# A Fourier filter and a token-mixing block on one core: the first batch redone in its first stage and its transposes, the first group moved ahead, and the planner's time from engine to engine cut to a quarter

## The chip, the cores and the metric

One core of one Trainium2 chip runs the whole kernel. Times are device microseconds (us) of one execution; a smaller one is better. The time before is the median of three runs, 1521.86 us (1519.93 to 1523.29).

## What is computed

```python
# x: (8, 3136, 256) float32; filters (1569, 256); w_ch1 (256, 1024), w_ch2 (1024, 256)
X = np.fft.rfft(x, axis=1)                       # along the 3136 tokens
y = np.fft.irfft(X * (filt_r + 1j * filt_i), n=3136, axis=1).astype(np.float32)

X = np.fft.fft(np.fft.fft(y, axis=1), axis=2)    # along tokens, then along 256 channels
u = y + np.real(X).astype(np.float32)
un = (u - mean(u)) / np.sqrt(var(u) + 1e-06)     # over the channels
out = u + np.maximum(un @ w_ch1, 0.0) @ w_ch2
```

## The kernel before

Each of the 8 batches is a transform, and the transform's result feeds the products of the block. A token axis of 3136 is split 112 x 28, so that every transform step is a product of TensorE. To keep float32 accuracy, a float32 value is held as a float16 pair (high part and rest), and each float32 product is three float16 products (high x high, high x rest, rest x high).

The steps of one batch `b`, with the line numbers of the profile:

- `load_x`, `measure_x`, `weigh_x`: seven loads of 448 KB; VectorE takes the absolute maximum of each (L387); a scale `sx`, a power of two, follows by a transpose and a product of TensorE in float32 (L364, L381).
- `first`, 14 chunks: ScalarE scales and rounds to the high part (L533), VectorE makes the rest (L535), TensorE does three products of 512 columns (L544), ScalarE and VectorE split the result into a pair (L549, L551), and a DMA stores 224 KB to DRAM tensor `d` (L554).
- `load_at`, seven pieces `ch`: `d` comes back in another order (L577). For batch 0 the tables `s2` and `i1` of the next steps are loaded in between (L582, L585).
- `spectrum`, two halves `hf` per piece: 16 small products (L618, L619), the filter on VectorE (L630, L634), the complex sums on GpSimd or VectorE (L641, L644, L646), the split into a pair (L653, L656 or L659), and a DMA transpose of the pair into `z` (L663). For batch 0, ScalarE scales the filters first (`scale_filters`, L457 to L462).
- `fold`: sums and differences of the halves (L682, L696), kept as pairs in `eo` (L708, L711) for the transform along the channels.
- `inverse1`, two per piece: six products (L732 to L734), split (L741, L743), store to DRAM (L746).
- `load_b2`, `inverse2`, `bring`: load (L760), products (L779), scale (L792), store to DRAM tensor `dy` (L803, L807).

The tokens of all batches are then one row of 49 groups of 256. For group `g`, `fetch` loads `y` (L825), `prepare` mixes the channels (L860, into `mix`), adds the result to `y` on VectorE (L870), takes mean and variance (L948, L949) and the weights of the normalisation (L952 to L964); `normalize` writes `un` (L977), splits it (L982, and L985 on VectorE for the first two groups) and sends it through a DMA transpose into `ut` (L991). `products` then makes 8 steps per group: a product `h` of six matmuls (L1013), the rectifier and its split (L1041, L1043), and two steps later 12 matmuls into `acc` (L1054). In all there are 392 steps. `weight` and `split_weights` turn the float64 weights, loaded as words in eight pieces (L1096), into float32 on VectorE and ScalarE (L1119 to L1135) and then into pairs (L1159 to L1163).

The order of the instructions on each engine isn't written out. A planner (`Plan`) runs all these steps as tasks in a time of its own: each task names an engine and a length, waits for events or for a buffer of a ring (`take`, `give`), and the engine that is free takes the waiting task with the lowest order number. The engines then work through the orders that came out, strictly one after another. `HOP` is what the planner adds when a task goes from one engine to another; `brought`, `FIRST` and `gate` tie the steps of later batches and groups to a step of `products`. Rings stand for the PSUM banks: `psf` (4 banks), `psh` (2, for `h`) and `pso` (2, for `acc`).

## Time and profile before

| what | us |
|---|---|
| device time, median of three | 1521.86 |
| device time of the profiled execution | 1524.17 |
| its span, first to last instruction | 1522.4 |
| TensorE busy in the span | 1379.6 (91%) |
| VectorE busy | 1114.9 (73%) |
| ScalarE busy | 784.4 (52%) |
| GpSimd busy | 541.5 (36%) |
| first product `h` begins at | 179.06 |

The profile shows one execution. Its lines by stretch give the busy time of each engine in that stretch, the clock that the throttle granted to TensorE (1.00 is 2.4 GHz, 0.50 is 1.2 GHz, a number between is a mean of the two), and the mean busy share and rate of the DMA engines. A line of the order of time gives the start, the length, the engine, the line of the code, what was written and read, and in brackets how long the engine sat idle just before and who ended it.

### The profile page before, as it was taken

The numbers are of one execution on the slowest core, as the hardware profiler recorded it, in microseconds if no ns is written. First come the engines' busy times: TensorE is split into PE (matmuls) and PEld (weight loads), VectorE is DVE, ScalarE is ACT, GpSimd is POOL, SyncE is SP. The second block draws the span as 40 slices with busy tenths as digits, with TensorE's granted clock in tenths as the row PEclk, the third lists the DMA queues.
The fourth block names the chain that finished last, engine by engine and source line by source line (L and its number), as shares of the span: only waits on it lengthen the run. The fifth ranks groups of instructions, "written<-read, shape, count | busy, mean of one in ns | idle before, by whom it ended". The sixth has DMA issues, their size and how long they took to land.

```text
span 1522.4 us, 29999 instructions
## 1 busy us (share of the span) xinstructions
PE 1379.6 (91%) x11217; PEld 935.0 (61%) x11217; DVE 1114.9 (73%) x2409; ACT 784.4 (52%) x1450; POOL 541.5 (36%) x675
## 2 busy tenths in 40 slices
PE   3442599999999999999999999999999999999998
PEld 1341257765776567666666666666666677666666
DVE  6774977787787877888688867878778878465563
ACT  4543565455464655565555545465455646443442
POOL 4461046501671038400860057211760167210100
PEclk9555589999999999999999999999999999999999
DMA  7999497956988698948987599758997698735521
GB/s 214 207 211 220 126 197 165 241 144 175 220 189 198 170 211 172 263 123 197 226 178 213 144 214 214 218 138 192 210 196 197 163 218 181 179 83 124 132 68 43
DMA packets 419827, 273.12 MB, mean 179 GB/s; under 512 B 234048, under 2 KB 361072, under 8 KB 419680
## 3 DMA queue, kind: packets, MB, share of 16 engines
q1 hardware_dynamic: 419680, 271.19, 77.0%
q8 instruction: 88, 1.44, 0.4%
q14 instruction: 59, 0.48, 0.1%
HBM read 113.31 MB, written 102.76 MB: 142 GB/s over the span
## 4 chain that ended last, share of the span: by engine, by line
PE 56%; DVE 4%; DMA 2%; issue 2%; ACT 1%; SPq 1%; POOL 1%; ACTq 0%; POOLq 0%; DVEq 0%
PE acc L1054 23%; PE h L1013 23%; PE y L779 3%; PE s L544 2%; PE mix L860 2%; DVE y L870 1%; PE i L732 1%; PE i L734 1%; PE i L733 1%; DMA ut<-u 1%; PE s L618 1%; PE s L619 1%; DMA b<-d 1%; DVE st L948 1%; DVE h L1043 1%
## 5 line engine op out<-in xcount | busy, mean ns | idle before, releaser
L1054 PE MATMUL acc<-w2s,h 128*128 128x256 f16 x4704 | 591.9, 273 | 2.8 <-DVE y L1068 2.7
L1013 PE MATMUL h<-ut,w1s 128*128 128x512 f16 x2352 | 578.0, 382 | 16.1 <-DMA ut<-u 11.6
L1054 PEld LDWEIGHTS <-h 128*128 128x128 f16 x4704 | 452.0, 98 | 142.3 <-issue 18.8
L1041 ACT ACTIVATE h<-h 128x512 f16<-128x512 f32 x392 | 233.5, 596 | 482.7 <-PE h L1013 481.9
L1043 DVE SCALAR_TENSOR_TENSOR h<-h,h 128x512 f16<-128x512 f32 x392 | 268.3, 684 | 213.9 <-ACT h L1041 213.1
L1013 PEld LDWEIGHTS <-w1s 128*128 128x128 f16 x2352 | 228.4, 98 | 222.9 <-issue 19.6
L988 POOL TENSOR_TENSOR u<-un,u 128x512 f16<-128x512 f32 x94 | 109.6, 1167 | 598.4 <-ACT u L982 524.6
L870 DVE SCALAR_TENSOR_TENSOR y<-mix,alpha,y 128x508 f32<-128x508 f32 (+1 forms) x368 | 160.5, 475 | 38.6 <-PE mix L860 33.4
L544 PE MATMUL s<-x,s 112*112 112x512 f16 x336 | 100.3, 425 | 20.6 <-ACT x L533 9.7
L644 POOL TENSOR_TENSOR yt<-yt,t 128x224 f32<-128x224 f32 x105 | 70.2, 668 | 134.3 <-DVE yt L636 83.4
L977 ACT ACTIVATE un<-y,sb 128x256 f32<-128x256 f32 x196 | 110.7, 595 | 12.5 <-DVE sb L964 8.5
L659 POOL TENSOR_TENSOR y<-yt,y 128x448 f16<-128x448 f32 x105 | 109.6, 1048 | 18.7 <-ACT y L653 15.4
L630 DVE TENSOR_TENSOR yt<-s,ft 128x448 f32<-128x448 f32 x112 | 69.1, 617 | 32.2 <-PE s L619 29.3
L535 DVE SCALAR_TENSOR_TENSOR x<-x,sx,x 112x512 f16<-112x512 f32 x111 | 86.9, 808 | 6.4 <-ACT x L533 6.3
L732 PE MATMUL i<-z,i 112*112 112x256 f16 x224 | 65.5, 292 | 25.2 <-DMA z<-y 20.1
L551 DVE TENSOR_TENSOR ast<-s,ast 112x512 f16<-112x512 f32 x112 | 74.5, 684 | 15.3 <-ACT ast L549 14.9
L711 POOL TENSOR_TENSOR eo<-ef,eo 128x448 f16<-128x448 f32 (+6 forms) x62 | 59.7, 966 | 71.8 <-ACT eo L708 71.6
L387 DVE TENSOR_REDUCE mx<-x 112x1 f32<-112x1024 f32 x56 | 67.5, 1211 | 23.6 <-DMA x<-x 23.6
L743 DVE TENSOR_TENSOR bt<-i,bt 112x512 f16<-112x512 f32 x112 | 74.8, 684 | 13.6 <-ACT bt L741 13.3
L948 DVE BATCH_NORM_STATS2 st<-y 128x6 f32<-128x256 f32 x196 | 80.8, 412 | 3.0
L792 ACT ACTIVATE ys<-y,alpha 128x512 f32<-128x512 f32 x112 | 73.4, 685 | 18.2 <-PE y L779 18.0
L544 PEld LDWEIGHTS <-s 112*112 112x112 f16 x336 | 46.3, 143 | 56.6 <-issue 37.1
(130 smaller groups left out, 1609.8 us busy)
## 6 DMA issues: line engine op xcount, KB each, us to landing
x<-x SPq DMA_DIRECT2D x56, 448.0 KB
d<-ast SPq DMA_DIRECT2D x112, 224.0 KB
at<-d SPq DMA_DIRECT2D x56, 448.0 KB
d<-bt SPq DMA_DIRECT2D x112, 224.0 KB
b<-d SPq DMA_DIRECT2D x56, 448.0 KB
out<-y SPq DMA_DIRECT2D x98, 256.0 KB
y<-dy SPq DMA_DIRECT2D x92, 256.0 KB
dy<-ys SPq DMA_DIRECT2D x96, 224.0 KB
```

Source lines behind the costliest of these rows:

```text
L535: nc.vector.scalar_tensor_tensor(x16[:, 1], x, sx[:112, 1:2], x16[:, 0], op0=ALU.mult, op1=ALU.subtract)
L544: nc.tensor.matmul(p, s1[:, hs], x16[:, hx], start=i == 0, stop=i == 2)
L659: nc.gpsimd.tensor_tensor(y16[:, :, 1, :112], ytv, y16[:, :, 0, :112], op=ALU.subtract)
L732: nc.tensor.matmul(p[:, i], i1[:, j + i, 0], z[:, i, 0], start=True, stop=False)
L870: nc.vector.scalar_tensor_tensor(out, p, al, y, op0=ALU.mult, op1=ALU.add)
L948: nc.vector.bn_stats(st[:, 2 * t + k], y[:, t, k])
L977: nc.scalar.activation(un[:, k], y[:, t, k], AF.Identity, bias=sb[:, i, 1:2], scale=sb[:, i, 3:4])
L988: nc.gpsimd.tensor_tensor(u16[:, :, :, 1], unv, u16[:, :, :, 0], op=ALU.subtract)
L1013: nc.tensor.matmul(p.rearrange("p (t k q) -> p t k q", t=2, k=2), w1s[:, d, hw, 128 * f : 128 * f + 128], utv[:, :, :, d, hx], start=i == ...
L1041: nc.scalar.activation(h[:, 0], p, AF.Relu)
L1043: nc.vector.scalar_tensor_tensor(h[:, 1], p, 0.0, h[:, 0], op0=ALU.max, op1=ALU.subtract)
L1054: nc.tensor.matmul(acc[:, kind], h[:, hh, c0 : c0 + 128], w2s[:, f, hw], start=f == 0 and kind == 0 and i == 0, stop=f == 7 and kind == 1 ...
```

## The change

1. **The planner.** `HOP` is 0.1 where it was 0.4.
2. **First stage of batches 0 and 1 in float32** (`WIDE = 2`). TensorE multiplies the loaded `x` itself by a float32 table `s1f`, one product per chunk, and the scale is applied when the result is split. The split of `x` (L533, L535) goes for these two batches. Chunks of batch 0 no longer wait for the scale; six PSUM banks of `psf` and `pso` and twelve buffers take their results.
3. **Filters.** They are no longer scaled by ScalarE; the filter operation on VectorE takes the scale as its scalar. What stays is a change of sign of a part (`conjugate`). Six of the eight filter measurements are on ScalarE, four before.
4. **Spectra of batch 0 turned on TensorE.** Four float32 transposes per half go to PSUM, and ScalarE and VectorE split from there into `z`. The 14 DMA transposes of batch 0 go, and with them the split of the spectra in SBUF. The later batches keep theirs.
5. **Tables.** They are loaded when the first-stage stores of batch 0 have been issued, ahead of `at`.
6. **Group 0 and the weights.** Group 0 is mixed as soon as its spectra are there, is normalised tile by tile, and has `pso` banks and low order numbers. Weights are loaded from the first `at` pieces on, four of the eight straight into the space of `w1s` and `w2s`. Batch 1 gets its order by hand: its first stage from step -7 on, its spectra from step 9 on.

Cut to its core, the diff reads:

```diff
+WIDE = 2
-FILTERS_ON_ACT = (0, 3, 4, 6)
-RAW_IN = ("ys", "ys", "b2", "ut", "ut", "ys", "b2", "ys")
+FILTERS_ON_ACT = (0, 2, 4, 5, 6, 7)
+RAW_IN = (None, None, "ys", "ys", "ut", "ut", None, None)
-HOP = 0.4
+HOP = 0.1
...
     def first(b, q, t):
+        ring = ("psf", "psf", "psf", "psf", "pso", "pso")[q % 6] if b == 0 else "psf"
+        wide = b < WIDE
...
+        if wide:
+            yield "PE", 0.86 if b else 1.2
+            nc.tensor.matmul(p, s1f, x, start=True, stop=True)
...
+            yield until(("sx", b))
...
         yield "ACT", 0.53
+        if wide:
+            nc.scalar.activation(st[:, :, 0], p, AF.Copy, scale=sx[:112, 1:2])
...
+        if wide:
+            nc.vector.scalar_tensor_tensor(st[:, :, 1], p, sx[:112, 1:2], st[:, :, 0], op0=ALU.mult, op1=ALU.subtract)
...
+    def load_tables():
+        for ch in range(7):
+            yield until(("fnyq",), *((("stored", 0),) if ch > 1 else ()))
+            yield "SP", 0.75, -101 if ch < 2 else -79
+            nc.sync.dma_start(s2[:, 8 * ch : 8 * ch + 8], a["c_s2"][:, 8 * ch : 8 * ch + 8])
...
+            nc.sync.dma_start(i1[:, 4 * ch : 4 * ch + 4], a["c_i1"][:, 4 * ch : 4 * ch + 4])
...
+        def filtered(out, p, f):
+            nc.vector.scalar_tensor_tensor(out, p, pF[:, 1:2], f, op0=ALU.mult, op1=ALU.mult)
...
+        if b == 0:
+            kp = yield take("psh")
+            pt = spare(f"yT_{ch}_{hf}")[:112].rearrange("p (j c) -> p j c", j=4)
+            yield "PE", 1.2
+            for j in range(4):
+                nc.tensor.transpose(pt[:, j], yt[:, hf, 112 * j : 112 * j + 112], ident)
...
+            yield "ACT", 0.53
+            nc.scalar.copy(z[:, :, 0], pt)
+            yield "DVE", 0.64
+            nc.vector.tensor_tensor(z[:, :, 1], pt, z[:, :, 0], op=ALU.subtract)
...
+        if g == 0:
+            yield until(("spectrum", 0, 6, 0), ("spectrum", 0, 6, 1))
+            kp, pm = yield from mixing()
...
+            if g == 0:
+                yield from weigh(slice(2 * t, 2 * t + 2))
+                plan.spawn(normalize(g, t, y, sb, ut), -56 + t)
...
+        x0, t0, s0, piece, half = ((-280, -100, -80, PIECE, HALF), (-30, -7, 9, 0.9, 1.25))[b] if b < 2 else (0,) * 5
```

How the rows of the engines move at the places that matter is shown word for word. On SyncE, which issues all DMAs, the end of the first stage of batch 0 stood like this before (`ast` are the stored chunks, `s` and `i` the tables, `at` the pieces that come back):

```order
L554 DMA d_0_168<-ast_13_375 112x1024
L577 DMA at_0_188<-d_0_168 112x8x256
L585 DMA i_83<-c_i 112x896
L577 DMA at_1_210<-d_0_168 112x8x256
```

and it stands like this now:

```order
L561 DMA d_0_133<-ast_13_274 112x1024
L596 DMA s_83<-c_s 112x896
L600 DMA i_84<-c_i 112x896
...
L596 DMA s_83<-c_s 112x896
L589 DMA at_0_144<-d_0_133 112x8x256
L589 DMA at_1_151<-d_0_133 112x8x256
L589 DMA at_2_158<-d_0_133 112x8x256
```

Nine tables of 196 KB now stand between the last store and `at_0`, where none stood.

On VectorE, between the last split of the first inverse step (`bt_6_1`) and the first addition of group 0 (`y`), before:

```order
L743 TENSOR_TENSOR bt_6_1_1026<-i_0_6_1_1008,bt_6_1_1026 112x2x256
L1119 TENSOR_SCALAR cv_3_1038<-raw_1033 128x512
L1121 SCALAR_TENSOR_TENSOR w_1037<-raw_1033,cv_3_1038 128x512
...
L387 TENSOR_REDUCE mx_1134<-x_6_1025 112x1
L508 TENSOR_REDUCE mx_1134<-mx_1134 112x1
L870 SCALAR_TENSOR_TENSOR y_118<-mix_1187,alpha_379,y_118 128x4x127
```

and now:

```order
L781 TENSOR_TENSOR bt_6_1_1025<-i_0_6_1_1004,bt_6_1_1025 112x2x256
L1190 SCALAR_TENSOR_TENSOR w_992<-raw_418,cv_2_993 128x512
L1192 SCALAR_TENSOR_TENSOR w_992<-raw_418,w_992 128x512
L1188 TENSOR_SCALAR cv_3_1036<-raw_472 128x512
...
L390 TENSOR_REDUCE mx_117<-x_5_968 112x1
L386 COPY sw_1183<-pb_w_1184 128x2
L390 TENSOR_REDUCE mx_117<-x_6_1024 112x1
L912 SCALAR_TENSOR_TENSOR y_119<-mix_920,alpha_307,y_119 128x4x127
```

The weight conversions there are those of the last six pieces now (18 long operations and 5 short ones, beside the seven maxima of batch 1), where three pieces stood before and the rest came after that addition.

On TensorE, around the first product `h` (`s_1_q` are the first-stage chunks of batch 1), before:

```order
L860 MATMUL mix_1227<-mix,eo 128x127
L544 LDWEIGHTS s_81
L544 MATMUL s_1_0_1276<-x_1_0_1238,s_81 112x512
...
L544 MATMUL s_1_5_1356<-x_1_5_1307,s_81 112x512
L1013 LDWEIGHTS w1s
L1013 MATMUL h_0_1384<-ut_1319,w1s 128x512
```

and now:

```order
L902 MATMUL mix_1233<-mix,eo 128x127
L384 MATMUL pb_x_1286<-row_x_1280,ones 128x2
L534 MATMUL s_1_0_1299<-x_0_922,s1f 112x512
...
L534 MATMUL s_1_6_1353<-x_3_925,s1f 112x512
L534 MATMUL s_1_7_1372<-x_3_925,s1f 112x512
L1080 LDWEIGHTS w1s
L1080 MATMUL h_0_1343<-ut_1204,w1s 128x512
```

Eight chunks of batch 1 stand ahead of the first `h`, six before, and each is one float32 product instead of three float16 ones.

## Rows read from the trace of the kernel before

**Rows 1.** By stretch, all engines: length; busy (x) of PE, PEld, DVE, ACT, POOL; clock, DMA.

```profile
0.00:20.00 20.00, 0.93 (x3) 0.74 (x4) 9.71 (x15) 2.49 (x5) 2.99 (x12) 1.00 0.92 260
...
60.00:80.00 20.00, 7.57 (x108) 7.16 (x108) 17.86 (x33) 10.69 (x23) 16.90 (x22) 0.50 1.15 230
80.00:100.00 20.00, 11.36 (x112) 10.43 (x112) 15.66 (x26) 9.08 (x18) 15.89 (x20) 0.67 1.11 235
...
200.00:220.00 20.00, 20.00 (x161) 13.33 (x160) 13.56 (x36) 9.01 (x18) 6.26 (x8) 0.88 1.05 219
```

**Rows 2.** In order of time, first stage of batch 0: start, length, engine, line.

```profile
19.75 0.16 DVE L383 COPY sx<-pb_x 128x2 f32<-128x2 f32 x1 [0.68 <-PE pb_x L381]
...
48.04 0.68 DVE L551 TENSOR_TENSOR ast<-s,ast 112x512 f16<-112x512 f32 x1
...
51.01 0.32 SPq L577 DMA_DIRECT2D at<-d  x1
...
55.28 0.23 PE L618 MATMUL s<-s,at 112*128 112x56 f16 x1 [8.64 <-DMA at<-d]
```

**Rows 3.** VectorE by line, 19 to 50 us: count, busy us, mean ns, idle before.

```profile
L535 DVE SCALAR_TENSOR_TENSOR x<-x,sx,x 112x512 f16<-112x512 f32 x13 | 13.8, 1076 | 0.8 <-ACT x L533 0.8
L551 DVE TENSOR_TENSOR ast<-s,ast 112x512 f16<-112x512 f32 x14 | 9.3, 685 | 2.2 <-ACT ast L549 2.1
```

**Rows 4.** VectorE by line, 55 to 119 us (spectra and first inverse step, batch 0).

```profile
L743 DVE TENSOR_TENSOR bt<-i,bt 112x512 f16<-112x512 f32 x14 | 9.3, 683 | 3.4 <-ACT bt L741 3.4
L630 DVE TENSOR_TENSOR yt<-s,ft 128x448 f32<-128x448 f32 x14 | 8.6, 616 | 5.2 <-PE s L619 4.9
...
L641 DVE TENSOR_TENSOR yt<-yt,t 128x224 f32<-128x224 f32 x7 | 5.0, 719 | 0.1
L696 DVE TENSOR_TENSOR ef<-yt 1x224 f32<-1x224 f32 x7 | 4.6, 663 | 4.8 <-POOL ef L682 4.7
L1121 DVE SCALAR_TENSOR_TENSOR w<-raw,cv 128x512 int32<-128x512 int32 x2 | 2.1, 1051 | 0.1
```

**Rows 5.** TensorE by line, 55 to 119 us.

```profile
L732 PE MATMUL i<-z,i 112*112 112x256 f16 x28 | 10.9, 390 | 23.3 <-DMA z<-y 18.3 <-DVE t L634 2.8 <-DVE bt L743 1.6
```

**Rows 6.** In order of time, 119 to 179 us, VectorE and one row of TensorE.

```profile
119.04 0.43 DVE L1119 TENSOR_SCALAR cv<-raw 128x512 int32<-128x512 int32 x1 [4.13 <-DMA raw<-w]
119.50 0.69 DVE L1121 SCALAR_TENSOR_TENSOR w<-raw,cv 128x512 int32<-128x512 int32 x1
...
123.78 1.92 PE L779 MATMUL y<-b,i 112*64 112x256 f16 x12 [10.27 <-DMA b<-d]
...
154.27 1.22 DVE L387 TENSOR_REDUCE mx<-x 112x1 f32<-112x1024 f32 x1 [2.23 <-DMA x<-x]
...
176.41 1.75 DVE L870 SCALAR_TENSOR_TENSOR y<-mix,alpha,y 128x508 f32<-128x508 f32 x4
178.20 0.43 DVE L948 BATCH_NORM_STATS2 st<-y 128x6 f32<-128x256 f32 x1
```

**Rows 7.** In order of time, TensorE: the first `h`, and the step it reaches at 205 us.

```profile
179.06 5.30 PE L1013 MATMUL h<-ut,w1s 128*128 128x512 f16 x12 [3.59 <-DMA ut<-u]
...
204.99 0.82 PE L1054 MATMUL acc<-w2s,h 128*128 128x256 f16 x6
```

**Rows 8.** TensorE by line and shape, 205 to 1500 us.

```profile
L1054 PE MATMUL acc<-w2s,h 128*128 128x256 f16 x4596 | 577.7, 273 | 2.8 <-DVE y L1068 2.7
L1013 PE MATMUL h<-ut,w1s 128*128 128x512 f16 x2293 | 560.4, 380 | 12.5 <-DMA ut<-u 8.0 <-DVE st L948 2.0 <-DVE y L870 1.6
...
L381 PE MATMUL pb_x<-row_x,ones 1*128 1x2 f32 x12 | 2.3, 256 | 0.0
L364 PE MATMUL pt_x<-ident,mx 112*1 112x112 f32 x6 | 1.6, 261 | 0.0
```

**Rows 9.** By stretch, TensorE alone: two of the stretches in which it stood.

```profile
360.00:370.00 10.00, 8.44 (x47) 0.83 0.31 107
...
520.00:530.00 10.00, 6.28 (x46) 0.95 1.13 231
```

More of the change, by code (lines that the diff above doesn't have):

```diff
@@ L106, in until, with set @@
         self.post(t, self.resume, task, None)
-    def set(self, event):
-        event.time = self.end
+    def set(self, event, now=False):
+        event.time = self.now if now else self.end
         for task, events in event.waiting:
@@ L360, in pow2 @@
         rows = col.shape[0]
-        k = yield take("psf")
-        pt = bank("pt_" + name)
+        ring, bank_ = ("psh", spare) if name in ("x0", "F") else ("psf", bank)
+        k = yield take(ring)
+        pt = bank_("pt_" + name)
         yield "PE", 0.3
@@ L377, in spread @@
         n = row.shape[1]
-        k = yield take("psf")
-        pb = bank("pb_" + name)
+        ring, bank_ = ("psh", spare) if name in ("x0", "F") else ("psf", bank)
+        k = yield take(ring)
+        pb = bank_("pb_" + name)
         yield "PE", 0.3
@@ L537, in first @@
             )
-        if q % 2:
-            give("big", 21 * b + q // 2)
-        kp = yield take("psf")
-        p = bank(f"s1_{b}_{q}")[:112].rearrange("p (n c) -> p n c", c=256)
-        yield "PE", 0.66
-        for i, (hs, hx) in enumerate(((0, 0), (0, 1), (1, 0))):
-            nc.tensor.matmul(p, s1[:, hs], x16[:, hx], start=i == 0, stop=i == 2)
-        give("x16", k)
-        k = yield take("ast")
-        st = fp.tile([112, 2, 2, 256], F16, tag="ast", name=f"ast_{b}_{q}", bufs=4)
+            if q % 2:
+                give("big", 21 * b + q // 2)
+        elif b or q > 5:
+            yield until(("sx", b))
@@ new lines, in first @@
+        kp = yield take(ring)
+        pool = {"psf": ps_f, "pso": ps_o}[ring]
+        p = pool.tile([128, 2, 256], F32, tag=ring, name=f"s1_{b}_{q}")[:112]
+        if wide:
+            yield "PE", 0.86 if b else 1.2
+            nc.tensor.matmul(p, s1f, x, start=True, stop=True)
+            firsts[b, q] = True
+            if (b, q ^ 1) in firsts:
+                give("big", 21 * b + q // 2)
+            yield until(("sx", b))
+            sx = sxs[b]
+        else:
+            yield "PE", 0.66
+            for i, (hs, hx) in enumerate(((0, 0), (0, 1), (1, 0))):
+                nc.tensor.matmul(p, s1[:, hs], x16[:, hx], start=i == 0, stop=i == 2)
+            give("x16", k)
@@ L556, in first @@
         done("d1", b, q)
+        firsts[b] = firsts.get(b, 0) + 1
+        if firsts[b] == 14:
+            plan.set(ev("stored", b), True)
+    firsts = {}
     def scale_up(b):
@@ L904, in prepare, with mixing @@
         yield until(*(("eo", b, c) for b, c in pieces(g, 224)), *((("i2",),) if g == 0 else ()))
+        tiles = [(256 * g + 128 * t, 256 * g + 128 * t + 128) for t in range(2)]
+        ring = "psf" if g else "pso"
+        def mixing():
+            kp = yield take(ring)
+            pm = bank(f"mix_{g}") if g else ps_o.tile([128, 512], F32, tag="pso", name="mix_0")
+            pm = pm.rearrange("p (t c) -> p t c", t=2)
+            for t, (g0, g1) in enumerate(tiles):
+                r0 = g0 % RING
+                yield "PE", 0.4
+                channels(pm[:, t], lambda e, h: eo[:, e, h, r0 : r0 + 128], t == 0, t == 1)
+            mixed[0] = 256 * g + 256
+            done("mixed", g)
+            return kp, pm
+        if g == 0:
+            yield until(("spectrum", 0, 6, 0), ("spectrum", 0, 6, 1))
+            kp, pm = yield from mixing()
         yield until(("y", g))
-        tiles = [(256 * g + 128 * t, 256 * g + 128 * t + 128) for t in range(2)]
         y = ys_of.pop(g)
@@ L913, in prepare @@
                     keep = mp.tile([128, 2, 256], F32, tag="un", name=f"keep_{g}", bufs=2)
-                    kn = yield take("psf")
+                    kn = yield take(ring)
                     row = slice(b * NS - g0, b * NS - g0 + 1)
-                    pn = bank(f"nyq_{g}_{t}")[row, :256]
+                    pn = bank(f"nyq_{g}_{t}") if g else ps_o.tile([128, 512], F32, tag="pso", name="nyq_0")
+                    pn = pn[row, :256]
                     yield "PE", 0.43
@@ L1177, in load_s1 @@
     def load_s1():
-        yield "SP", 0.3
+        yield "SP", 0.3, -300
+        nc.sync.dma_start(s1f, a["c_s1f"])
+        done("s1f")
+        yield "SP", 0.3, -60
         nc.sync.dma_start(s1, a["c_s1"])
@@ L1188, in _program @@
         plan.spawn(measure_filters(q), -150)
-    for ch in range(7):
-        plan.spawn(scale_filters(ch), -60 + 3 * ch)
+    for q in range(4, 8):
+        plan.spawn(conjugate(q), -88)
     for i in range(8):
@@ L1204, in _program @@
         for q in range(14):
-            plan.spawn(first(b, q, t0 + PIECE * q), t0 + PIECE * q)
+            plan.spawn(first(b, q, t0 + piece * q), t0 + piece * q)
         plan.spawn(load_at(b, s0 - 2), s0 - 2)
```

290 lines of the change are left out of this document (145 added, 145 removed).

## Prediction

> **What bounds the kernel now.** I read the stretches first [rows 1]. From 200 us on TensorE is busy all the time at a granted clock that soon reads 1.00; before that it is mostly idle or at 0.50, and VectorE and the DMA engines carry the work. So there are two parts with different limits: a start of some 200 us, in which batch 0 goes through its transforms and group 0 is made, and then 1317 us of TensorE at work. A microsecond saved in the start is a microsecond off the end; one saved off TensorE in the second part is nothing.
>
> In the start, the first scale of x is known at 19.91 us, the last chunk of the first stage leaves VectorE at 48.72, its reload is issued at 51.01, and the first spectrum begins at 55.28 [rows 2]. The inverse step that follows waits above all for DMA transposes, 18.3 us of its 23.3 us [rows 5]. The first `h` begins at 179.06, and at 204.99 TensorE is in the second `acc` step [rows 7]. In these 25.9 us it has done four `h`, eight chunks of batch 1, eight matmuls of `y` and 12 of `acc`. From the means of 256 and 512 columns [rows 8] a column costs (380 - 273) / 256 = 0.42 ns and a matmul a constant 166 ns that overlaps with the next, so this work is worth 4 x 6 x 0.215 + 8 x 3 x 0.215 + about 1 for `y` + 12 x 0.107 = 12.6 us. Some 13.3 us were lost there, to waits and to the low clock.
>
> The steps of the change therefore have to be followed to one date, the first `h`, and from there to the date at which TensorE is full.
>
> **Part 1, the first stage of batch 0.** Removed: the split of x on VectorE, 13.8 us [rows 3], and its ScalarE half. A float32 product takes the place of three float16 ones. Its price no row shows at this size. A float32 transposition of 112 columns lasts 261 ns; less the constant, that is 0.85 ns a column, twice a float16 column; and a float32 product is recorded as two instructions (12 for six scales) [rows 8]. So 512 columns cost 2 x 512 x 0.85 = 0.87 us at the full clock and 1.74 us at half. The bounds are 0.65 us, three float16 passes, and 2.4 us, two times the whole 261 ns scaled to 512 columns; I take 1.74 in this cold stretch. Six products fit in front of the scale. Eight are left, each waiting for a bank that VectorE frees: 19.9 + 1.3 (first split, 0.69 on VectorE and as much ahead on ScalarE) + 8 x 1.74 + 1.3 = 36.4 us for the last split, against 48.7 (bounds 31, where VectorE alone would set it, and 42).
>
> A rule of the Trainium skill speaks against this edit: its page "FP8 and Floating Point Precision", in "TensorE Precision Notes", counts four passes for a true float32 product, so one more than the three it replaces. By that rule a chunk would be an estimated four float16 products, 0.86 us at the full clock, and the sum would stay as it is; no run here shows a float32 product of this size.
>
> **Part 2, the tables.** Nine tables of 196 KB, 1.8 MB, now stand ahead of the reload on SyncE. At 260 GB/s, the rate of the first 20 us [rows 1], that is 6.9 us, of which 2.3 us would pass anyway, while the last store lands (48.72 to 51.01). The reload then takes its 4.3 us (51.01 to 55.28): 36.4 + 2.3 + 4.6 + 4.3 = 47.6; I take 49, as the first-stage stores and filters share the same engines. First spectrum 6 us earlier (bounds 42 and 54).
>
> **Part 3, spectra to the end of the inverse step.** DMA transposes and their wait go. VectorE's list is now: 14 splits of the inverse step and 14 splits of the transposed spectra, priced by the same PSUM row, 28 x 0.683 = 19.1; 28 filter operations x 0.616 = 17.2; seven sums x 0.719 = 5.0; seven edges x 0.663 = 4.6 [rows 4]; some 2 us of small ones as before; and six long and three short operations of the weights, 6 x 0.87 + 3 x 0.43 = 6.5, taken between 0.69 [rows 6] and 1.05 [rows 4]. Sum 54.4 us. VectorE was never denser here than 17.9 of 20 us [rows 1]; at that share the list lasts 61 us, so the last split leaves at 110. The ends are 54 us, no gap at all, and 70 us, the 15.7 of 20 of the next stretch. TensorE's own list is shorter even at half clock: per piece 32 spectrum matmuls, 12 of 256 columns at 0.21 and eight transposes at some 0.22 make below 6 us, seven pieces 42. GpSimd loses seven splits.
>
> On the 1.05 the profile and the skill can be read together: the weight operation lasts 0.69 at 119 us and 1.05 between 55 and 119 us, where GpSimd is busy up to 16.9 of 20 us [rows 1, 4, 6]; the operations with one operand in PSUM stay at 0.68 there. The Trainium skill's page "SBUF — State Buffer", in "SBUF: two separate sides", says that VectorE with two SBUF inputs and GpSimd exclude each other for a whole instruction, which fits these rows. By that rule the change's new splits, which read PSUM, are not slowed.
>
> **Part 4, to the first `h`.** Ahead of the first addition of group 0, VectorE now has 18 long weight operations x 0.69, five short x 0.43, seven maxima x 1.22 [rows 6] and some 3 us of small ones: 26.1, with gaps between dependent ones 27 us, so 137. Hidden behind that is the path of `y`: reload of the inverse (4.3), product (1.9), scale (1.4), store and fetch (4.3 each) are 16 us. In the run before, batch 1's loads went in between, and its last maximum, at 154.27, still stood ahead of that addition; now these loads are ahead. Were the weights not there, `y` would be the limit, at 126.
>
> Then VectorE alone counts. Tile 0: addition 1.75, the odd first token 1.3, two statistics of 0.43 and 0.18, five weights of 0.2 and a root on ScalarE 0.7: 6.0. Tile 1: 1.75, 1.2, 1.7, a split of 0.7 and 0.7, batch 1's scale 1.9, a piece of group 1's addition 1.1: 9.0. That is 15 us (its two additions and a statistic in [rows 6]), so the last split of group 0 leaves at 152; its transposes land by 156. But TensorE comes to `h` only after chunk 7 of batch 1, and chunk 7 needs the bank that chunk 3 leaves. VectorE reaches that after two chunks, both additions and statistics of group 1, its weights and two more chunks: 4 x 0.69 + 2.4 + 2.4 + 1.0 = 8.6, with gaps 9. First `h` at 152 + 9 + 1 = 162, against 179.06: 17 us earlier.
>
> **Part 5, after it.** w2 is ready now, where before the second `acc` step came only at 205. Of the 13.3 us lost I leave 4 (bounds 2 and 10), for the low clock and the crowd of chunks on VectorE: 9 us gained. The rest of TensorE's work is the same: six chunks x 0.87 = 5.2 after the first `h`, where eight x 0.65 = 5.2 stood. Filters unscaled cost the later batches nothing, as the filter operation reads PSUM at the same length.
>
> **Part 6, the planner.** With `HOP` at 0.1 it believes that results come sooner, and orders closer. In the run before, TensorE stood 12.5 us ahead of `h` between 205 and 1500 us, and 2.8 ahead of `acc` [rows 8], most where few steps lie between a group's mixing and its `h`: six steps at group 12, and 3.7 us lost in 520 to 530 [rows 9]. Before, groups 12, 21 and 35 have six. Now groups 3 and 6 have five, and none has six. I take the sum as unchanged, with -10 and +15 as ends.
>
> **Sum.** 17 + 9 = 26 us less. The profiled execution, 1524.2 us with its 1.8 us around the span, becomes 1498; it lies 2.3 us above the median of the runs, so 1496.
>
> **The rivals.**
> *More than that.* VectorE packs its list without gaps in part 3 (-7), the loss after `h` is 2 us (-2), and at best the float32 products run at the full clock (-5): 1482 to 1487, down to 1476 with fewer stands later. For it: nothing waits for a transpose any more. Against: 80 to 100 us shows 15.7 of 20.
>
> *Less: the gain is given back at group 6.* Batch 1's spectra begin at the 10th `h` now, at the 6th before, while group 6, the first with tokens of batch 1, keeps its 49th. In the run before, TensorE already stood 1.6 us at 360 to 370 us for it [rows 9]. Four steps are 4 x 3.4 = 14 us (1317 us for 388 steps): 1510. The DMA engines, with eight weight pieces, tables and batch 1 ahead of the reload, come to the same only if they fall 15 us behind the run before: with the product at its old 123.78 [rows 6] `y` would be there at 134, still ahead of the 137 of part 4.
>
> *No change.* The start shortens, but the first `h` waits for w1, whose last split on ScalarE and GpSimd now comes late, or the planner's order gives back what the start gained: 1520.
>
> *Slower.* The tight order makes `h` wait for its transpose in every group after the first. The price is the 1.6 us of 360 to 370 us [rows 9], for 47 groups 75, less the 8.0 already there [rows 8]: 1496 + 67 = 1563. It decides from 0.55 us a group on (26 / 47).
>
> **How the numbers follow.** Chances: the forecast, 1488 to 1505, 0.48; more, 0.20; less, 1505 to 1518, 0.19; no change 0.04; slower 0.09. A measurement can tell about 0.2%, 3 us. Faster 0.87, same 0.04, slower 0.09. The range leaves out the slower rival and the outermost ends: 1476 to 1517.
>
> **What will show it.** The last split of the first stage near 36 us and the first spectrum near 49; no wait of the inverse step for a DMA; VectorE at 0.9 or more from 50 to 160 us; the first addition of group 0 near 137, the first `h` near 162 and the first `acc` a few us later; stands of about 15 us ahead of `h` and `acc` after it, at groups 3 and 6 first. Wrong would be: VectorE with wide gaps between 50 and 110, a first `h` after 172, or `h` waiting for its transposes in most groups.

## The result and the profile after

| | before | after |
|---|---|---|
| median, us | 1522.57 (1519.93 to 1528.86) | 1463.57 (1461.17 to 1464.24) |
| ratio | | 0.9604 (95% interval 0.9572 to 0.9636) |
| span of the profiled execution, us | 1522.4 | 1461.1 |
| mean granted clock of TensorE | 0.950 | 0.971 |

The changed kernel is 59 us faster. (The kernel before has a fourth run here, so its median is 1522.57 and not 1521.86; the ratio is taken over the runs, the quotient of the two medians is 0.9613.) The forecast was 26 us faster, 1496, with a range from 1476 to 1517: the sign is right, and the time lies below the range.

The start has dates that can be followed in both traces; step k is the k-th product `h`, counted from 0.

| date, us | before | forecast | after |
|---|---|---|---|
| last split of the first stage ends | 48.7 | 36.4 | 33.1 |
| first spectrum | 55.3 | 49 | 44.6 |
| last split of the first inverse step ends | 114.9 | 110 | 94.5 |
| first addition of group 0 | 155.6 | 137 | 118.2 |
| first `h` | 179.1 | 162 | 145.4 |

The rows of after in order of time, TensorE and VectorE (start, length, engine, line; in brackets the idle time before and who ended it), answer to [rows 2, 6, 7]:

```profile
6.07 8.20 PE L534 MATMUL s<-x,s1f 112*112 112x512 f32 x12 [6.07 <-DMA x<-x]
...
32.30 0.75 DVE L556 SCALAR_TENSOR_TENSOR ast<-s,sx,ast 112x512 f16<-112x512 f32 x1 [0.24 <-ACT ast L551]
...
44.61 0.23 PE L635 MATMUL s<-s,at 112*128 112x56 f16 x1 [8.89 <-DMA at<-d]
...
93.78 0.68 DVE L781 TENSOR_TENSOR bt<-i,bt 112x512 f16<-112x512 f32 x1
94.39 0.68 DVE L1190 SCALAR_TENSOR_TENSOR w<-raw,cv 128x512 int32<-128x512 int32 x1
...
118.24 0.72 DVE L912 SCALAR_TENSOR_TENSOR y<-mix,alpha,y 128x508 f32<-128x508 f32 x1
...
145.35 4.21 PE L1080 MATMUL h<-ut,w1s 128*128 128x512 f16 x12
```

The first six products now run while x still loads. The weight operation at 94.39 starts 0.07 us before the split ahead of it has ended (93.78 + 0.68); that overlap matters below. By stretch, all engines, as in [rows 1]:

```profile
60.00:80.00 20.00, 11.72 (x153) 9.96 (x153) 19.86 (x36) 8.72 (x16) 15.82 (x21) 0.92 0.87 265
80.00:100.00 20.00, 9.71 (x78) 8.59 (x76) 19.29 (x33) 10.92 (x23) 9.57 (x10) 0.67 0.79 229
100.00:120.00 20.00, 7.35 (x42) 3.57 (x42) 19.17 (x41) 14.77 (x32) 3.00 (x3) 0.59 0.71 200
```

VectorE (the third engine) is busy for 19.86 of 20 us where it was at 17.86, and stays above 19 up to 120 us. TensorE alone, in four stretches that end at the first `h`, at step 12 and at step 44, of before and then of after (length, busy, clock, DMA share, GB/s):

```profile
0.00:179.06 179.06, 66.83 (x449) 0.65 0.80 200
179.06:232.40 53.34, 49.78 (x343) 0.82 0.85 183
232.40:342.10 109.70, 108.07 (x919) 1.00 0.77 183
342.10:1522.40 1180.30, 1154.95 (x9512) 1.00 0.77 176
```

```profile
0.00:145.35 145.35, 72.54 (x491) 0.73 0.78 224
145.35:184.90 39.55, 39.55 (x285) 0.96 0.72 181
184.90:303.00 118.10, 114.64 (x981) 0.99 0.83 199
303.00:1461.10 1158.10, 1144.49 (x9494) 1.00 0.74 178
```

The 61.3 us between the spans are 33.7 up to the first `h`, 13.8 from there to step 12, and 13.8 after it (22.2 less 8.4: more of batch 1 is done before step 44 now, 6.6 us busy, and so less behind it). After step 12 TensorE stood 27.0 us before and 17.1 now, and the other 4 us are busy time, some of it at half clock (9.4 us of TensorE's work before, 3.0 now). The longer stands after step 44 by who ended them (us, times, the longest), of before and then of after:

```profile
PE h L1013 <- DMA ut<-u: 8.0, 6, 2.7
PE acc L1054 <- DVE y L1068: 2.5, 5, 0.9
...
PE s L544 <- DVE x L535: 0.9, 2, 0.5
...
```

```profile
PE h L1080 <- DMA ut<-u: 5.8, 4, 3.5
PE s L543 <- DVE x L522: 2.1, 6, 0.6
PE acc L1121 <- DVE y L1135: 1.3, 3, 0.9
...
```

### The profile page after: what moved, and what is told of

Read it like the earlier page. It is cut to its first block, busy times and chain, and to the rows that moved or that the text cites. A ratio compares the mean times of both kernels' runs of the same rounds, so it can differ in the third digit from the quotient of the medians.

```text
span 1461.1 us, 29950 instructions
## 1 busy us (share of the span) xinstructions
PE 1371.2 (94%) x11245; PEld 932.3 (64%) x11245; DVE 1108.6 (76%) x2391; ACT 764.2 (52%) x1407; POOL 522.1 (36%) x660
## 3 DMA queue, kind: packets, MB, share of 16 engines
q8 instruction: 88, 1.44, 0.4%
## 4 chain that ended last, share of the span: by engine, by line
PE 52%; DVE 3%; DMA 1%; ACT 1%; issue 0%; POOL 0%; ACTq 0%; DVEq 0%
PE acc L1121 22%; PE h L1080 21%; PE y L817 2%; PE s L543 2%; PE mix L902 1%; DVE y L912 1%; PE i L770 1%; PE s L635 1%; PE s L636 1%; PE i L771 1%; PE i L772 1%; DMA ut<-u 1%; DVE h L1110 0%; DVE st L1025 0%; DVE y L1135 0%
## 5 line engine op out<-in xcount | busy, mean ns | idle before, releaser
L1121 PEld LDWEIGHTS <-h 128*128 128x128 f16 x4704 | 451.2, 98 | 136.8 <-issue 12.6
L1080 PEld LDWEIGHTS <-w1s 128*128 128x128 f16 x2352 | 227.9, 98 | 209.1 <-issue 12.3
L1044 ACT ACTIVATE un<-y,sb 128x256 f32<-128x256 f32 x196 | 111.5, 595 | 25.7 <-DVE sb L1005 17.9
L668 POOL TENSOR_TENSOR yt<-yt,t 128x224 f32<-128x224 f32 x98 | 64.5, 658 | 124.8 <-DVE t L654 114.1
L697 POOL TENSOR_TENSOR y<-yt,y 128x448 f16<-128x448 f32 x98 | 101.2, 1035 | 7.9 <-ACT y L695 7.6
L654 DVE SCALAR_TENSOR_TENSOR t<-s,pF,ft 128x448 f32<-128x448 f32 x126 | 84.1, 674 | 9.2 <-PE s L636 9.2
L654 DVE SCALAR_TENSOR_TENSOR yt<-s,pF,ft 128x448 f32<-128x448 f32 x98 | 66.4, 677 | 28.6 <-PE s L636 25.5
L779 ACT CAST bt<-i 112x512 f16<-112x512 f32 x112 | 65.3, 585 | 31.1 <-PE i L772 27.6
L1135 DVE SCALAR_TENSOR_TENSOR y<-acc,beta,y 128x512 f32<-128x512 f32 x98 | 69.8, 743 | 9.3 <-PE acc L1121 9.0
L635 PE MATMUL s<-s,at 112*128 112x56 f16 x896 | 62.3, 190 | 13.8 <-DMA at<-d 8.9
L817 PE MATMUL y<-b,i 112*64 112x512 f16 (+1 forms) x480 | 63.0, 381 | 11.1 <-DMA b<-d 11.1
```

Source lines behind the costliest of these rows:

```text
L635: nc.tensor.matmul(o, w, s2[:, U, 0].rearrange("p (r k) -> p r k", r=2), start=True, stop=False)
L654: nc.vector.scalar_tensor_tensor(out, p, pF[:, 1:2], f, op0=ALU.mult, op1=ALU.mult)
L697: nc.gpsimd.tensor_tensor(y16v[:, 1], yh, y16v[:, 0], op=ALU.subtract)
L817: nc.tensor.matmul(p[64 * h : 64 * h + 64, js], i2[:, i_, h, i], bt[:, 2 * o + js.start : 2 * o + js.stop, h], start=i == 0, stop=i == 1,)
L1044: nc.scalar.activation(un[:, k], y[:, t, k], AF.Identity, bias=sb[:, i, 1:2], scale=sb[:, i, 3:4])
L1080: nc.tensor.matmul(p.rearrange("p (t k q) -> p t k q", t=2, k=2), w1s[:, d, hw, 128 * f : 128 * f + 128], utv[:, :, :, d, hx], start=i == ...
```

## The experiments

All were timed against the kernel before, each set on one chip. Ratios, with their 95% intervals, compare across sets; an interval is some 0.25% wide to either side, so two ratios that differ by less than 0.4% (6 us) are not told apart by them. Dates come from one profile each.

| run | median, us | ratio | first spectrum | last inverse split | first addition | first `h` | step 12 | span |
|---|---|---|---|---|---|---|---|---|
| changed kernel | 1463.57 | 0.9604 (0.9572 to 0.9636) | 44.6 | 94.5 | 118.2 | 145.4 | 184.9 | 1461.1 |
| e1 | 1482.26 | 0.9748 (0.9723 to 0.9773) | 41.3 | 98.8 | 119.3 | 143.1 | 181.4 | 1480.6 |
| e2 | 1504.6 | 0.9892 (0.9869 to 0.9915) | 55.4 | 113.0 | 154.0 | 178.1 | 226.0 | 1505.3 |
| e3 | 1479.62 | 0.9731 (0.971 to 0.9752) | 55.2 | 103.4 | 130.5 | 149.2 | 190.4 | 1477.7 |
| e4 | 1478.12 | 0.9717 (0.9698 to 0.9736) | 42.9 | 100.2 | 136.8 | 154.5 | 195.2 | 1474.7 |
| e5 | 1459.7 | 0.9598 (0.9568 to 0.9629) | 40.8 | 98.3 | 119.1 | 142.4 | 182.2 | 1457.5 |
| e6 | 1454.74 | 0.9558 (0.9532 to 0.9584) | 39.4 | 90.8 | 116.9 | 137.4 | 177.8 | 1452.5 |
| e7 | 1464.17 | 0.9623 (0.9595 to 0.9651) | 44.6 | 94.8 | 119.9 | 139.0 | 179.5 | 1460.9 |
| e8 | 1463.48 | 0.9617 (0.9593 to 0.9641) | 41.2 | 94.6 | 119.0 | 140.7 | 179.4 | 1461.2 |
| e9 | 1465.7 | 0.963 (0.9609 to 0.9651) | 44.1 | 99.6 | 121.3 | 140.7 | 188.9 | 1463.7 |
| e10 | 1463.1 | 0.9615 (0.9596 to 0.9634) | 45.7 | 94.9 | 120.2 | 146.1 | 184.2 | 1464.1 |
| e11 | 1471.44 | 0.967 (0.9652 to 0.9687) | 44.1 | 94.0 | 119.1 | 139.9 | 187.7 | 1469.2 |
| e12 | 1461.83 | 0.9603 (0.9587 to 0.9619) | 41.4 | 96.3 | 120.0 | 142.2 | 181.0 | 1459.4 |
| e13 | 1458.12 | 0.9598 (0.9572 to 0.9624) | 44.4 | 94.3 | 120.5 | 142.8 | 181.9 | 1456.3 |
| e14 | 1466.87 | 0.9652 (0.963 to 0.9675) | 44.6 | 94.8 | 130.2 | 150.8 | 189.8 | 1464.9 |
| e15 | 1452.42 | 0.955 (0.9528 to 0.9573) | 40.3 | 91.8 | 118.2 | 135.7 | 176.7 | 1450.2 |

### The planner's HOP: e1, e2, e8, e5

```diff
-HOP = 0.1
+HOP = 0.4
```

> The changed kernel with the planner's HOP back at 0.4; nothing else differs. Theory A (two gains that don't need each other: the start, first h at 145.4 and TensorE full at once, 46 us by the 12th step; and some 14 us later, from the shorter HOP, because TensorE stands 13 us less and falls to half clock less often): first h stays within 3 us of 145, the stands after it come back, time 1463.6 + 14 = 1477. Rival B (HOP does nothing later; the new kernel stands less because its start leaves every later batch in another phase): first h at 145, time 1463 to 1466. Rival C (HOP made the start dense as well): first h at 155 or later, time 1487 or more.

In the old kernel the other way round:

```diff
-HOP = 0.4
+HOP = 0.1
```

> The kernel before with HOP at 0.1 alone; the whole start is the old one. Theory A: first h within 3 us of 179, some 14 us fewer after it, time 1522 - 14 = 1508. Rival B: 1519 to 1525. Rival C: the first h moves ahead by 10 us or more, time below 1500.

Theory A holds in both: a HOP of 0.1 is worth 1.44% in the new kernel and 1.08% in the old one (some 22 and 16 us, where A had said 14), and the first `h` moves by 2.3 and 1.0 us. C falls by those dates; B, because the old start gains as well. The loss of e1 lies behind step 44, which it reached at 292.7 (the changed kernel at 303.0) and from where it needs 1187.9 us to the end (1158.1); e2 needs 1167.6, the old kernel 1180.3. One stand of e1 shows where most of its loss sits. TensorE and VectorE of e1 in order of time:

```profile
309.23 0.38 PE L543 MATMUL s<-x,s 112*112 112x512 f16 x1
318.02 2.57 PE L543 MATMUL s<-x,s 112*112 112x512 f16 x5 [8.40 <-DVE x L522]
```

```profile
310.87 1.78 DVE L912 SCALAR_TENSOR_TENSOR y<-mix,alpha,y 128x508 f32<-128x508 f32 x4
...
313.77 1.75 DVE L912 SCALAR_TENSOR_TENSOR y<-mix,alpha,y 128x508 f32<-128x508 f32 x4
...
317.22 0.74 DVE L522 SCALAR_TENSOR_TENSOR x<-x,sx,x 112x512 f16<-112x512 f32 x1
```

TensorE holds one third of a chunk and stands 8.4 us for the rest half of x. ScalarE had finished the high part by 308.5, but in VectorE's order the split stands behind all additions and statistics of a group. The same happened at 821 us (5.6 us). Behind step 44 stands of this kind come to 14.8 us in e1, and to 2.1 in the changed kernel, where the longest is 0.6:

```profile
PE s L543 <- DVE x L522: 14.8, 4, 8.4
```

That is the larger part of the 17.9 us by which TensorE stands longer there in e1. The old kernel lost its time in other places: at the same HOP it had 0.9 us of this kind. What fell there with a HOP of 0.1 (e2) is the wait for `ut`, from 8.0 us to 1.1:

```profile
PE h L1013 <- DMA ut<-u: 1.1, 1, 1.1
```

That a short HOP gains behind step 44 is shown in both kernels. Which stands it removes differs with the start, and why is not shown.

> The changed kernel with HOP at 0.2, between the two. Theory A (a shorter HOP gives fewer stands, step by step): time 1468 to 1472, a third of the 19 us given back, idle time of TensorE after the first h 14 to 18 us (10.6 at 0.1, 27.5 at 0.4, stands over 0.3 us). Rival F (chance of the order): no line between the ends, 1460 or 1480 as likely.

The time misses: 0.9617 cannot be told from 0.9604. The stands over 0.3 us, 15.7 us in sum, lie where A had them, and two things cancel in the time: behind step 44 it needs 1168.2 us, between e1 and the changed kernel, but it reaches that step at 293.0, 10 us sooner.

```diff
+        self.hop = 0.4
...
+                if q == TIGHT_FROM:     # 36
+                    plan.hop = HOP      # 0.1
```

> The changed kernel with HOP at 0.4 up to the 36th step of the products and 0.1 from there on. TensorE's order up to there is that of e1, which reached the 44th step at 292.7 us (the changed kernel: 303.0) and then lost 29 us to the end. Theory A' (the two halves add: the planner's short HOP is worth some 29 us after the 44th step and costs 10 before it): 44th step at 293 +- 2, 1158 us from there to the end, time 1463.6 - 10 = 1453. Rival F (each later order is a matter of chance, and the order after step 36 comes out with stands of any size): time anywhere from 1460 to 1480, stands above 20 us.

The second half comes out as A' says, 1159.7 us behind step 44. The gain ahead of it does not: step 44 came at 297.8, and the time cannot be told from the changed kernel's. F falls, as stands over 0.3 us sum to 13 us. So the gain of a short HOP behind step 44 was seen with three starts (e2, e5, the changed kernel). How much of such a difference may be chance can be read off as well: the thirteen kernels here that have the new code, whole or in most parts, and a HOP of 0.1 from step 44 on need between 1158.1 and 1166.7 us from there to the end. The 1187.9 us of e1 lie far outside; the 1168.2 of e8 lie hardly outside. Of the 10.3 us by which the changed kernel comes to step 44 later than e1, 3.5 are there at step 12, and in between it does 5.0 us more work (114.64 us busy against 109.64). With a HOP of 0.1 and another place of the tables (e6) step 44 comes at 292.6.

### The first stage: e3, e7

```diff
-WIDE = 2
+WIDE = 0
...
-        yield "SP", 0.3, -60
+        yield "SP", 0.3, -300
         nc.sync.dma_start(s1, a["c_s1"])
```

> The changed kernel with the first stage of batches 0 and 1 in three float16 products again (WIDE = 0, and the float16 table loaded first); transposes on TensorE, tables, group 0 and HOP stay changed. Theory A (the first stage was bound by VectorE's split of x, 13 operations of 1.08 us, and by the wait for the scale): the last split of the first stage leaves at about 46 instead of 33, everything behind it moves by the same, first h at 158, time 1476. Rival D (the tables and the DMA engines set the first spectrum, not the first stage): first spectrum at most 4 us later, first h at 149, time 1467.

> The changed kernel with the first stage in float32 for batch 0 alone (WIDE = 1); batch 1 makes pairs and three float16 products. It splits e3, which was 16 us slower, into batch 0 and batch 1. Theory A (batch 0's chunks are what counts, their 13.8 us of VectorE and the wait for the scale; batch 1's split costs VectorE 14 times 0.7 to 1.1 us, half of it after the first h, where TensorE has other work): first h within 3 us of 145, time 1463.6 + 4 = 1468. Rival H (VectorE is the bound up to the 12th step, so every split counts in full, in either batch): 12th step at 195 instead of 185, time 1473 or more.

`WIDE = 1` costs nothing that the ratio can tell; `WIDE = 0` costs 1.27%. So the gain needs batch 0's chunks, and batch 1's add none that the ratio can tell. H falls (step 12 at 179.5, sooner than in the changed kernel). A's first `h` missed: in e7 it comes 6.3 us sooner, with two chunks of batch 1 ahead of it instead of eight. In e3 the first spectrum is 10.6 us later and the first addition 12.3, so D falls and A's dates hold so far, but the first `h` comes only 3.8 later: three chunks of batch 1 stand ahead of it there instead of eight. The rest is paid later: 5.5 us at step 12, 10.9 at step 44, 16.6 at the end. The first `h` by itself is no date.

### The transposes: e4

```diff
-        if b == 0:
+        if b == 0 and TURNED:      # False
             kp = yield take("psh")
```

(what follows for later batches then serves batch 0 too, with the rest of the second halves made on VectorE, as in the kernel before)

> The changed kernel with the spectra of batch 0 made into pairs in SBUF and turned by DMA transposes again; the rest stays changed. Theory A (VectorE was at 17.9 of 20 us before because the inverse step waited 18 us for these transposes, and is at 19.9 now because it no longer does): TensorE waits for z<-y again for over 10 us in the inverse step, VectorE falls to 0.9 there, first h at 155 to 158, time 1473 to 1476. Rival E (VectorE is dense for another reason, the tight order and the filters that left ScalarE): VectorE's list is 2 us shorter, since 14 splits of 0.68 us go and 7 of 1.07 us come, first h at 143 to 146, time 1461 to 1464.

Theory A: step 12 comes 10.3 us later, and the time is 1.13% longer. TensorE's wait and VectorE's gaps are back (waits of 43 to 100 us, and VectorE alone by stretch):

```profile
PE i L775 <- DMA z<-y: 12.2, 4, 4.0
```

```profile
60.00:80.00 20.00, 17.61 (x28) 0.59 1.08 219
80.00:100.00 20.00, 16.40 (x24) 0.59 0.87 202
```

That is close to the 17.86 and 15.66 of [rows 1]. E falls: the density of VectorE came from the transposes.

### The tables: e6

```diff
-            yield until(("fnyq",), *((("stored", 0),) if ch > 1 else ()))
+            yield until(("fnyq",), *((("at", 0, ch),) if ch > 1 else ()))
...
-            yield until(("stored", 0))
+            yield until(("at", 0, ch))
```

> The changed kernel with eight of the nine tables behind the pieces of the reload again (one ahead of the first at, as s2 needs it). Theory A, by the sum on record (nine tables cost 4.6 us ahead of the reload, and VectorE is dense from the first spectrum on): first spectrum at 40 to 41 instead of 44.6, the end 4 us earlier, 1459. Rival G (the tables are needed soon after anyway: VectorE or TensorE then waits for them between 45 and 60 us, and each at piece queues behind a table): first spectrum at 41, VectorE below 0.9 in 60 to 80 us, the last split of the inverse step where it was or later, time 1463 to 1468.

The first spectrum comes 5.2 us sooner (4.6 in the prediction's sum), step 12 7.1 and the end 8.6 in the profiles; the ratio is lower by 0.46%, just what the ratios can tell. A, and more than A; G falls, as VectorE is busy 19.35 of 20 us from 60 to 80. The same edit on the kernel of e13 (e15, below) gives 0.48%. So this part of the change was a loss, but only with the short HOP: when the planner starts with a HOP of 0.4 or 0.2 (e1, e5, e8), two tables stand between the last store and the reload instead of nine, and the first spectrum comes at 40.8 to 41.3. SyncE in e8:

```profile
32.95 0.38 SPq L561 DMA_DIRECT2D d<-ast  x1
33.38 0.49 SPq L600 DMA_DIRECT2D i<-c_i  x1
33.92 0.51 SPq L596 DMA_DIRECT2D s<-c_s  x1
36.16 0.33 SPq L589 DMA_DIRECT2D at<-d  x1
```

### Does VectorE's list set the date? e9, e10

```diff
-            yield "DVE", 0.64
+            yield "DVE", 1.28
+            nc.vector.tensor_tensor(z[:, :, 1], pt, z[:, :, 0], op=ALU.subtract)
             nc.vector.tensor_tensor(z[:, :, 1], pt, z[:, :, 0], op=ALU.subtract)
```

> The changed kernel with VectorE's split of the turned spectra of batch 0 done twice (14 operations of 0.68 us more, 9.5 us; the second writes what the first wrote). Theory A (VectorE's list alone sets the dates from the first spectrum to the first h): the last split of the inverse step at 103 instead of 94.5, the 12th step of the products 9.5 us later, time 1473. Rival J (VectorE only looks full: TensorE, the reload or the inverse's way through DRAM sets the dates, and the planner puts other work in): 12th step at most 3 us later, time 1464 to 1467.

The same with `nc.scalar.copy(z[:, :, 0], pt)` and ScalarE's 1.06:

> The same doubling on ScalarE: its cast of the turned spectra, 14 operations of some 0.63 us more, 8.8 us. ScalarE is busy 8.7 and 10.9 of 20 us in 60 to 100 us. Theory A: the cast stands in the chain of each half but not on the engine that is full, 12th step at most 2 us later, time 1463 to 1466. Rival K (the chain of one half, not VectorE's list, is what bounds): as much as the other doubling, 1470 or more.

ScalarE's doubling changes nothing (K falls). VectorE's does less than A said: of 9.5 us the last inverse split shows 5.1, the first addition 3.1, step 12 4.0 (J had at most 3) and the profiled end 2.6. The time lies in J's range and can't be told from the changed kernel's. VectorE stays dense, but the planner moves work: 21 long weight operations stand between the last inverse split and the first addition instead of 18, and all chunks of batch 1 stand behind the first `h`. So VectorE's list counts for these dates, by about half at the last inverse split, and a microsecond on it is not a microsecond at the end.

### From the inverse step to the first addition: e11, e13, e14

```diff
     def load_x(b, t):
         yield gate(t)
+        if b == 1:
+            yield until(("placed", 0, 1))
```

> The changed kernel with the loads of batch 1 held back until the second piece of y is stored, as in the kernel before; the planner then puts two of batch 1's maxima ahead of group 0's first addition (seven before the change and after it), and the first three h ahead of batch 1's chunks. Theory A (the early loads only took the maxima's wait for x off VectorE; with two maxima ahead the addition is as early as now): first addition at 118 +- 4, first h at 135, chunks of batch 1 between the first steps, 12th step at 185 +- 4, time 1460 to 1468. Rival L (the late loads were what held the old kernel's addition at 155.65, 40.8 us behind the last split of the inverse step, where it is 23.7 now): first addition at 130 or later, time 1475 or more.

The addition comes at 119.1 (A's date), but the time is 0.66% longer, half-way to L. The chunks of batch 1 now lie behind the first `h`; step 12 is 2.8 us later, but step 44 only 1.2. Of the 8.1 us at the end 7.0 lie behind step 44, where the thirteen kernels differ by up to 8.6 us anyway, so this run does not decide between A and L.

```diff
-        plan.spawn(fetch(g), 8 * g + FIRST - 3 if g else -56)
-        plan.spawn(prepare(g), 8 * g + FIRST if g else -55)
+        plan.spawn(fetch(g), 8 * g + FIRST - 3)
+        plan.spawn(prepare(g), 8 * g + FIRST)
```

(and `normalize` and `urgent` likewise)

> The changed kernel with group 0's order numbers as before the change (fetch -16, preparation -13, normalisation -7, and the first two pieces of y by their old due time); loads of batch 1 stay early, tile-by-tile work and PSUM banks stay. All seven maxima and all weight operations then stand ahead of its first addition on VectorE. Theory N (the 40.8 us between the last split of the inverse step and that addition in the kernel before came from the loads of batch 1 standing late; with the loads early the maxima find their data): first addition at 122 +- 4, time 1464 to 1468. Theory O (it is the place in the order that counts): first addition at 130 or later, time 1472 or more.

> Both: group 0's order numbers as before and the loads of batch 1 behind the second piece of y, so that the addition stands behind seven maxima that wait for their data, as in the kernel before. Theory N: the addition falls back by the whole 17 us, to 135 or later, time 1478 or more. Theory O: as e13, within 3 us.

O falls: the place of group 0 in the order is worth nothing that the ratio can tell (0.9598 against 0.9604). With all seven maxima ahead of the addition, late loads move it from 120.5 to 130.2, step 44 by 7.5 us, and cost 0.54%. N's direction is right; its size, 17 us, is not. The rows of the kernel before say where the rest was: what VectorE waited for longest between 95 and 156 us there,

```profile
DVE mx L387 <- DMA x<-x: 11.4, 7, 6.7
DVE cv L1119 <- DMA raw<-w: 7.3, 3, 4.1
DVE row_w L367 <- PE pt_w L364: 3.4, 1, 3.4
...
```

and in the changed kernel between 94 and 119 us:

```profile
DVE w L1198 <- ACT cv L1196: 0.3, 1, 0.3
```

The words of the weights were waited for as well as x. That early weights have the other part is argued from these rows; no run took them back.

### Put together: e12, e15

> A version meant to beat both: tables behind the reload as in e6 (1454.7), HOP at 0.2 up to the 44th step (e8 reached it 10 us before the changed kernel) and 0.1 from there on (as e5, whose second part kept the 1159 us of the changed kernel). Theory A (VectorE's list sets the start, so an earlier first spectrum and a better order there share the same slack only in part): 44th step at 286 to 292, time 1447 to 1454. Rival M (both gains are the same slack): 1454 to 1458. Rival F (chance): above 1460.

> e6 and e13 together: the tables behind the pieces of the reload and group 0's order numbers as before the change. Each alone was faster than the changed kernel, by 8.8 and 5.5 us. Theory P (they take time from different places: the tables from the date of the first spectrum, the order from the stand of TensorE ahead of the first h): first spectrum at 39 to 40, first h at 135, time 1449 to 1452. Rival Q (the start has some 8 us of slack that either one uses up): 1454 to 1457. Rival F (an order of this kind moves the end by some 5 us for no reason that a single edit has): 1457 or more.

e12 is no faster than the changed kernel, as F had it. Its first spectrum came at 41.4 and e8's at 41.2: with a HOP of 0.2 only two tables stood ahead of the reload in any case, so their place had little left to give. Step 44 came at 292.7, and from there it needed 1166.7 us, where A had counted on 1159; it is the slowest of the thirteen there. e15 can't be told from e6 (0.955 against 0.9558). P's first `h` came (135.7), the time lies between the ranges of P and Q, and whether e13's edit adds anything to e6 is not settled. e6 and e15 are the fastest here, some 0.5% under the changed kernel.

## Why the prediction was wrong

The start was read rightly as a part in which time can be gained, and the sign followed. The second part, taken as full, had time to give too. The miss, 1498 for the profiled execution against 1462.9, is 35 us, in six terms. Seen with e1, it falls into two: at the old HOP the rest of the change took 41.8 us off the span, where parts 1 to 5 had 26, and the shorter HOP took the other 19.5, where part 6 had nothing.

**Part 1, the clock of the first stage: 3.3 us.** The price per clock was right. TensorE in the changed kernel, in order of time, around the scale and behind step 3:

```profile
21.59 4.28 PE L534 MATMUL s<-x,s1f 112*112 112x512 f32 x5 [1.76 <-DVE ast L556]
```

```profile
25.14 5.03 PE L534 MATMUL s<-x,s1f 112*112 112x512 f32 x11
```

```profile
159.23 1.02 PE L534 MATMUL s<-x,s1f 112*112 112x512 f32 x2
160.09 1.46 PE L1080 MATMUL h<-ut,w1s 128*128 128x512 f16 x6
```

A chunk is two instructions; the two rows share the one at 25.14, in which the clock rose. At half clock the starts of two instructions lie 0.85 us apart, 1.71 a chunk (1.74 forecast); at full clock they lie 0.43 apart, and at 159 us the next product starts 0.86 after the chunk (0.87 forecast). What failed is "in this cold stretch". TensorE by stretch, of after and then of before:

```profile
18.60:25.40 6.80, 4.39 (x7) 0.50 0.99 335
25.40:34.00 8.60, 5.19 (x12) 1.00 0.93 314
```

```profile
20.00:30.00 10.00, 6.40 (x14) 1.00 0.62 214
30.00:40.00 10.00, 6.48 (x17) 1.00 0.39 119
```

The half clock that I took is the 0.50 of 60 to 80 us in [rows 1]; between 20 and 40 us the first stage had run at 1.00 before the change as well, and I took no row of that stretch. The eight products behind the scale took 9.0 us instead of 13.9, so the clock was worth 4.9; 0.4 of it went at their start and 1.2 behind the last product, where the splits waited for ScalarE. Four passes for a float32 product, as the Trainium skill has it ("FP8 and Floating Point Precision", "TensorE Precision Notes"), agree with the 0.86 us: four float16 products of 512 columns at the 0.215 us of the prediction. That is dearer than the 0.65 of three, and speaks against the edit only where TensorE is the bound.

**Part 2: 1.1 us.** 11.6 us from the last split to the first spectrum, 12.6 forecast. The DMA engines moved 304 GB/s between 20 and 40 us, not 260. That the tables cost some 5 us there was right (e6: 5.2).

**Part 3, VectorE's list: 11.1 us, the largest term in the start.** 49.9 us, 61 forecast. Its rows in the changed kernel, 44.6 to 94.5 us:

```profile
L654 DVE SCALAR_TENSOR_TENSOR t<-s,pF,ft 128x448 f32<-128x448 f32 x28 | 17.9, 672 | 9.2 <-PE s L636 9.2
L687 DVE TENSOR_TENSOR z<-yT,z 112x512 f16<-112x512 f32 x14 | 9.4, 678 | 0.9 <-ACT z L685 0.9
L781 DVE TENSOR_TENSOR bt<-i,bt 112x512 f16<-112x512 f32 x14 | 9.4, 679 | 0.5 <-ACT bt L779 0.4
L734 DVE TENSOR_TENSOR ef<-yt 1x224 f32<-1x224 f32 x7 | 3.7, 535 | 0.6 <-POOL ef L720 0.6
L665 DVE TENSOR_TENSOR yt<-t,t 128x224 f32<-128x224 f32 x7 | 2.9, 411 | 0.1
L1192 DVE SCALAR_TENSOR_TENSOR w<-w1s,w 128x512 int32<-128x512 int32 x2 | 2.1, 1046 | 0.0
```

Most of the 9.2 us of idle time ahead of L654 lies before 44.6; inside the stretch VectorE stood 3.2 us. Two mistakes stand in the step that makes 61 us of 54.4 by 17.9 of 20. The larger one is the list: it was a sum of durations, while the 17.9 is busy time without double counting. Neighbouring instructions overlap (0.07 us at 94.39), so counts times means of this view add up to 53.0 us, and VectorE's busy time in 44.61 to 94.46 is 46.70: 7.7 us under the 54.4, of which 1.4 are prices. The other is the density. It was taken from a stretch whose gaps were in large part the very wait that the change removes, as e4 brings wait and gaps back together: 6.6 us of gaps were allowed, 3.2 came, so 3.4 us. Of the prices, sums (0.411) and edges (0.535) were put at 0.719 and 0.663, from a stretch in which GpSimd was busier (16.90 and 15.89 of 20 us, against 15.82 and 9.57); that this is the reason no run tests. The filter operations, with the scale as their scalar, took 0.672 where 0.616 stood. The splits that read PSUM kept their 0.68, as forecast, and L1192 with both inputs in SBUF its 1.05.

**Part 4: 1 us.** 23.8, 16.1 and 11.1 us where 27, 15 and 10 stood. That the sum is so near is partly luck, as 3.2 too much stands against 1.1 and 1.1 too little; the list behind the 27 was again a sum of durations. And the terms say less than they seem to: e9 shows that the planner fills in.

**Part 5: 4.8 us.** "I leave 4" of the 13.3 lost behind the first `h`, and the row of 145.35 to 184.90 shows no idle time and a clock of 0.96. The gain to step 12 is 13.8 us. It is the start's, as e1 with the old HOP needs 38.3 us for the same steps.

**Part 6, HOP: 13.8 us behind step 12, the largest step of all.** "I take the sum as unchanged" is the step that failed: it counted the steps from mixing to `h` and put the planner's constant itself at nothing. e1 and e2 give 1.4% and 1.1% for HOP alone. The 13.8 us are what is left of two things: from step 12 to the end the new kernel needs 1299.2 us with the old HOP (e1), 9.2 more than the old kernel, and 1276.2 with the new one. Ahead of step 12 the short HOP costs the new kernel 3.5 us, with the tables ahead of the reload. The places I chose to watch, groups 3 and 6 with five steps from mixing to `h`, waited 0.2 us for `ut` in all; the two long waits came at 761 us (3.48) and 980 us (1.80), at groups 22 and 30, which are mixed more steps ahead than groups 3 and 6. I read a longer lead as the only thing that helps and did not ask what a HOP does to the order on VectorE, as at 318 us of e1. The end of -10 was too near.

Of the rivals, "more" came nearest, its reasons first (a packed list, little loss behind `h`), its end 12 us too high, because it gave the planner little. "Less", "no change" and "slower" didn't come about: `h` waited for its transposes for 5.8 us in all.

## What to carry to other kernels

Price a list by the engine's busy time and not by the sum of durations, and take its density from no stretch whose gaps the change itself removes. Where a planner's constant changes, look at what each engine's order lets pass the operation that another engine waits for next, and don't take "the same work in another order" as zero: here it was worth 1.1 to 1.4%. With a planner, compare two starts at a step by which the same work is done: the first `h` alone can come early with work left behind it. And let several kernels show how far the rest differs without a reason (8.6 us here) before a smaller difference is put down to an edit.
